# Forward transforms of three long convolutions in three F32R passes, with the first norm's x loaded in kernel row order

## The chip, the cores and the metric

The kernel runs on one core of one Trainium2 chip. The metric is the device time of one execution, in microseconds (us). A core has five engines that run side by side, each on its own list of instructions: TensorE (PE, with its weight loads shown apart as PEld), VectorE (DVE), ScalarE (ACT), GpSimd (POOL) and SyncE (SP). They wait for each other only where a semaphore says so. Transfers are issued by SP's and POOL's queues here and run on 16 DMA engines.

## The reference

One transformer-like block over 2048 rows of 576 channels: a norm with modulation, a long convolution (S4D) computed with FFTs, a residual, a second norm with modulation, a dense layer with ReLU (576 to 4608 to 576), a residual. All in float32.

```python
x = A_u
mod = (_silu(c) @ w_mod).reshape(c.shape[0], 6, 1, -1)
sa, ca, ga, sb, cb, gb = ...
h = _layernorm(x) * (1 + ca) + sa
# _A_ref: K[d, l] = 2 Re sum_n C exp(A dt l);  y = irfft(rfft(h) * rfft(K))[:L];  y + h * D_skip
x = x + ga * _A_ref(h, ...)
h = _layernorm(x) * (1 + cb) + sb
x = x + gb * (maximum(h @ w1, 0) @ w2)
```

## The kernel before

**Blocks.** The 2048 rows are four blocks of 512. For each block s there is a convolution `conv(s)` and a feed-forward part (FFN) of 36 groups, g = 36 s to 36 s + 35, 128 hidden channels each. A group is 14 products of 512 columns into `hps` (L1368), a ReLU on ScalarE (`hh`, L1373), the rest of it on VectorE (`hl`, L1374), and 14 products into the sums `acc` (L1394). Both FFN factors are split into high and low parts of type F32R, and a product is three passes: high times high, high times low, low times high. From group 110 on, the FFN's first half takes another form with 256-column products (`first2`, L1495).

**Order of the work.** conv(0) runs ahead of the FFN. What belongs to the later blocks is put between the FFN's products: `step`, called four times a group (144 steps a block), pulls pieces from a generator. Under block 0's FFN lie the kernel rotations of `rest` (the convolution kernels of the later blocks, L486 to L521) and then conv(1); under block 1's lie `finish(0)`, more of `rest`, and conv(2); under block 2's lie `finish(1)` and conv(3). A piece yields its estimated VectorE time, or `None` for a piece of TensorE work. A step pulls while the time pulled in the block is below `rate(b)` times the number of the step, while the last four steps have pulled less than 7.5 us (block 0) or 7.0 us, and at most two TensorE pieces. At the end of a block the rest is issued at once. The lists are then laid out by the scheduler of the Tile layer, which may reorder an engine's work; instructions wrapped in `Kept` keep their program order among themselves.

**The convolution.** conv(s) loads x of its block (`x2`, rows in the order m, n with row 4 m + n) and one of two kernel tiles `kt`, computes the first norm into `h` (`norm1`: statistics L903, two scalings L937 and L938), and transforms both by matrices: for each half p of the channels, `mm_K` transforms kernel rows with the table `fcK`, `mm_U` transforms `h` with `fcU`. One such call is `transform` (L847): eight float32 matmuls of 128 x 128 by 288 columns into `ps_f` (L854), each copied to `Z` on ScalarE (L855). There are four calls a convolution, interleaved with the butterflies (`butterfly`, L860 to L883) of the call before. The tables differ since the kernel rows lie in another order on the partitions than x: place j holds row group 8 (j mod 16) + j // 16. Then come the products over earlier blocks (`product`, L1034 to L1040, with tiles `T`), the inverse transforms into x (`inverse`, L1061, L1066), the second norm, transposes (L1155), and the split into `xh`, `xl`, `xs` (L1159 to L1168), on which the next block's FFN begins.

**Memory.** Big tiles of a convolution come from a ring of seven S tiles (`spec`, 9216 bytes a partition), small ones from two T tiles (`half`). The memory of the rings is opened anew for each convolution, on the place where the tables of `rest` were.

**Queues.** SP's queue carries the FFN's weights. POOL's queue carries x, the kernel tiles, the stored spectra (`Ud`, `Kd`, `Rd`) and the outputs, in program order where they are `Kept`.

Of the kernel before, what the change touches and what calls it, by code (L numbers as in the profile page):

```python
# [18 lines left out]
P = 128  # L19
# [556 lines left out]
class Body:  # L576
# [34 lines left out]
    def early(self, kg):  # L611

        nc, I, sm = self.nc, self.I, self.sm
        x2 = self.x2[0] = self.x2p[0].tile([P, 4, D], F32, tag="x2", bufs=1, name="x2_0")
        nc.sync.dma_start(out=x2, in_=I["x"][0:512, :].rearrange("(m n) d -> m n d", n=4))
        self.fcU, self.fcK, self.gc = (
            sm.tile([P, 4, 2, P], F32, name=n) for n in ("fcU", "fcK", "gc")
        )
        for t, n in ((self.fcK, "fck"), (self.fcU, "fcu"), (self.gc, "gc")):
            nc.sync.dma_start(out=t, in_=I[n])  # L620
        kept = self.tc.keep_in_program_order
        self.mv1 = mv = sm.tile([P, 4, 5], F32, name="mv1")
        for i in range(4):
            yield
            st = sm.tile([P, 2, 6], F32, tag="st", bufs=8, name="st0")
            for p in range(2):
                kept(nc.vector.bn_stats(out=st[:, p], in_=x2[:, i, p * PC : (p + 1) * PC]))
            kept(nc.vector.bn_aggr(out=mv[:, i, 0:2], in_=st))
        yield
        kept(nc.scalar.activation(mv[:, :, 2], mv[:, :, 1], AF.Sqrt, bias=self.eps))  # L630
        yield
        kept(nc.vector.reciprocal(mv[:, :, 3], mv[:, :, 2]))
        kept(nc.vector.scalar_tensor_tensor(
            mv[:, :, 4], mv[:, :, 0], -1.0, mv[:, :, 3], op0=ALU.mult, op1=ALU.mult
        ))
        self.h0 = h = kg.pw.tile([P, 4, D], F32, tag="W2", bufs=5, name="h_0")
        for i in (0, 2, 1, 3):
            kept(nc.scalar.activation(
                h[:, i], x2[:, i], AF.Identity, scale=mv[:, i, 3:4], bias=mv[:, i, 4:5]
            ))  # L640
        yield
        self.kt0 = kg.kt0
        kept(self.skip(self.kt0, 0, nc.vector))
        for i in (0, 2, 1, 3):
            kept(nc.vector.tensor_tensor(h[:, i], h[:, i], self.m["ca"], op=ALU.mult))
            kept(nc.vector.tensor_tensor(h[:, i], h[:, i], self.m["sa"], op=ALU.add))
        self.wm = {}
        for nm in ("sb", "cb"):
            self.wm[nm] = kg.pw.tile([P, 5, D], F32, tag="W2", bufs=5, name=f"wm_{nm}")
        yield  # L650
# [121 lines left out]
    def main(self, ctx, kg, hooks):  # L772
# [11 lines left out]
        def block0():  # L784
            self.x2p.append(self.pool(ctx, "x2b"))
            yield from kg.rest(
                self.cps, {h: (1, 2, 3) if h < 6 else (1,) for h in (0, 6, 1, 7, 2, 8, 3, 9, 4, 10, 5, 11)}
            )
            self.xp.append(self.pool(ctx, "xb"))
            pool(1)  # L790
            yield from self.conv(1)

        def block1():
            yield from self.finish(0)
            yield -1
            self.cvs.close()
            yield from kg.rest(self.cps, {h: (2, 3) for h in range(6, NH)})
            pool(2)
            yield from self.conv(2)

        def block2():
            yield from self.finish(1)
# [122 lines left out]
    def norm1(self, x2, h):  # L925
# [9 lines left out]
        for i in range(4):  # L935
# [2 lines left out]
            f(h[:, i], h[:, i], mv[:, 3:4], self.m["sa"], op0=ALU.mult, op1=ALU.add)  # L938
            yield 1.6

    def conv(self, s):

        nc = self.nc
        v = self.vec.tensor_tensor
        xp = self.xp[s % 2]
        if s:
            x2 = self.x2p[s % 2].tile([P, 4, D], F32, tag="x2", bufs=1, name=f"x2_{s}")
            self.x2[s] = x2
            Kept(self.tc, nc.gpsimd).dma_start(
                out=x2,  # L950
                in_=self.I["x"][s * 512 : (s + 1) * 512, :].rearrange("(m n) d -> m n d", n=4),
            )
        else:
            x2, h = self.x2[0], self.h0
            self.fcKn, self.gcn = (
# [8 lines left out]

        kt = [kernel_tile(0) if s else self.kt0, None]
        yield -1 if s else "mod"
        if s:
            h = self.spec(f"h_{s}").rearrange("p a b c -> p a (b c)")
        hv = h.rearrange("m n (dd p q) -> m n dd p q", dd=4, p=2)

        def mm_U(p, Z):
            return self.transform(lambda n2: hv[:, n2, :, p], self.fcU, Z, s == 0)

        def mm_K(p, Z):
            ktv = kt[p].rearrange("p (t dd g) q -> p t dd g q", t=2, g=2)
            if s == 0 and p == 1:
                self.skip(kt[p], p, Kept(self.tc, nc.gpsimd))
            src = lambda n2: ktv[:, n2 // 2, :, n2 % 2]
            if s == 0 and p == 1:
                return self.transform1(src, self.fcK, self.fcKn, Z)  # L980
            return self.transform(src, self.fcK, Z, s == 0)
# [112 lines left out]
            yield from mm_K(1, ZK)  # L1094
            self.save(self.Rd[0][0], Ks[0], Kept(self.tc, nc.gpsimd))
        else:
            yield from both(self.norm1(x2, h), mm_K(0, ZK))
            kt[1] = kernel_tile(1)
            ZU = self.spec("Z")
            yield from both(spec_K(0, ZK), mm_U(0, ZU))  # L1100
# [603 lines left out]
            yield  # L1704

    def rate(self, b):
        return (2.15, 1.8, 1.4, 0.5)[b]


def after(n, g):  # L1710
# [19 lines left out]
def _layout(inputs):  # L1730
# [3 lines left out]
    perm = np.arange(D).reshape(4, 2, 3, 2, 12).transpose(1, 2, 3, 0, 4).reshape(-1)  # L1734
    r = {}
    r["x"] = a["A_u"].reshape(L, D)
    for k, s in (("lar", "A_log_A_real"), ("ai", "A_A_imag")):
        x = a[s][perm].reshape(NH, H, N).transpose(1, 0, 2)
        r[k] = np.concatenate([x, np.zeros((KR - 2 * H, NH, N), x.dtype), x])
# [50 lines left out]
```

## Time and profile before

| | us |
|---|---|
| runs: median of 3 (lowest to highest) | 1319.47 (1313.34 to 1321.47) |
| the profiled execution | 1324.17 |
| its span, first to last instruction | 1322.4 |
| its mean granted TensorE clock | 0.943 |
| busy: PE, PEld, DVE, ACT, POOL | 1210.1, 973.6, 993.3, 518.8, 161.1 |

The profile is of one execution. Its views used here: the chain of work that ended last, busy time of each engine in chosen stretches (times from the span's start), groups of equal instructions, and single instructions in order of time. A group's row has, after the shapes and the count, its busy us and the mean ns of one, then the idle time before it with what ended it. In a row of the timeline, start and length come first, and the bracket at the end tells how long the engine had been idle and who released it. Matmuls overlap in the records, so that a single one looks longer than it costs; what one costs is read from a run of many.

### The profile page before, as it was taken

Reading aid. Unit: us, or ns where it says so; the run is one execution under the profiler, and the core shown is the slowest. Engines: PE = TensorE matmul, PEld = TensorE weight load, DVE = VectorE, ACT = ScalarE, POOL = GpSimd, SP = SyncE. Lnnn points to the kernel's source line nnn. Section 1 sums busy time; section 2 is a strip of 40 time slices with the busy share of each in tenths; the row PEclk is TensorE's granted clock in tenths of the full one; section 3 lists DMA queues with packets and bytes.
Section 4 is the critical chain, followed back from the end, with each engine's and each line's share of the span. In section 5 each row is a group of like instructions: output and inputs, shape, how many; then the busy total and the mean of one; then the engine's idle time right before and its main releaser. Section 6 shows DMA issues by size and latency. Waiting matters only on the chain.

```text
span 1322.4 us, 27077 instructions
## 1 busy us (share of the span) xinstructions
PE 1210.1 (92%) x11094; PEld 973.6 (74%) x11094; DVE 993.3 (75%) x1538; ACT 518.8 (39%) x902; POOL 161.1 (12%) x256
## 2 busy tenths in 40 slices
PE   4665586899989998999999999999999999999998
PEld 3454464677767787787677887887888888998997
DVE  7899988999986999689468995467997237555543
ACT  5788423222223422622243225433222365434431
POOL 1676411011000100110001000100000000000000
PEclk9556787999989999999899999999999999999999
DMA  9758972988878967799779995877996658666641
GB/s 273 269 201 307 327 275 79 351 289 321 312 267 294 344 228 274 249 405 343 251 266 340 348 353 155 274 220 263 373 388 191 180 166 256 190 190 190 193 142 63
DMA packets 118032, 343.81 MB, mean 260 GB/s; under 512 B 17772, under 2 KB 21652, under 8 KB 107156
## 3 DMA queue, kind: packets, MB, share of 16 engines
q1 hardware_dynamic: 101332, 226.04, 51.0%
q0 software_dynamic: 16064, 114.67, 22.9%
q8 instruction: 87, 1.43, 0.4%
q10 hardware_dynamic: 512, 1.38, 0.3%
q14 instruction: 37, 0.30, 0.1%
HBM read 260.63 MB, written 81.40 MB: 259 GB/s over the span
## 4 chain that ended last, share of the span: by engine, by line
PE 71%; DVE 16%; DMA 7%; issue 3%; ACT 1%; POOL 1%; SPq 0%; ACTq 0%; DVEq 0%
PE acc L1394 28%; PE hps L1368 21%; PE hps L1495 7%; PE ps_f L854 5%; DMA L1d<-w 4%; PE kps L73 2%; PE kps L521 2%; PE ps_i L1061 2%; PE ph L73 2%; DVE T L486 1%; DVE W1r L488 1%; DMA x<-in_x_dram 1%; DVE Y L1040 1%; DVE T L64 1%; DVE w L1338 1%
## 5 line engine op out<-in xcount | busy, mean ns | idle before, releaser
L1394 PE MATMUL acc<-w,hh 128*128 128x512 f32 x1008 | 323.1, 403 | 3.2 <-ACT hh L1373 2.7
L1368 PE MATMUL hps<-xh,w 128*128 128x512 f32 x880 | 307.4, 410 | 0.7 <-ACT xh L49 0.7
L1394 PEld LDWEIGHTS acc<-w,hh 128*128 128x128 f32 x1008 | 187.4, 188 | 44.0 <-ACT hh L1373 3.6
L1368 PEld LDWEIGHTS hps<-xh,w 128*128 128x128 f32 x880 | 168.6, 192 | 38.7 <-ACT xh L49 1.3
L1394 PE MATMUL acc<-w,hl 128*128 128x512 f32 x504 | 195.1, 401 | 1.5 <-DVE hl L1374 1.5
L1343 ACT ACTIVATE w<-r 128x576 fp32r<-128x576 f32 x141 | 96.6, 685 | 229.7 <-PE acc L1394 195.2
L1368 PE MATMUL hps<-xl,w 128*128 128x512 f32 x440 | 175.7, 400 | 0.0
L1373 ACT ACTIVATE hh<-hps 128x512 fp32r<-128x512 f32 x110 | 65.7, 597 | 242.1 <-PE hps L1368 237.4
L1374 DVE SCALAR_TENSOR_TENSOR hl<-hps,hh 128x512 fp32r<-128x512 f32 x110 | 75.4, 685 | 113.1 <-ACT hh L1373 112.5
L1394 PEld LDWEIGHTS acc<-w,hl 128*128 128x128 f32 x504 | 94.3, 189 | 22.8 <-DVE hl L1374 3.0
L1333 ACT ACTIVATE w<-r 128x640 fp32r<-128x640 f32 x124 | 90.8, 732 | 42.7 <-DMA L1d<-w 42.1
L1368 PEld LDWEIGHTS hps<-xl,w 128*128 128x128 f32 x440 | 84.1, 191 | 18.3 <-DVE xl L49 0.4
L1040 DVE TENSOR_TENSOR Y<-Y,T 128x1152 f32<-128x1152 f32 x60 | 79.3, 1348 | 0.0
L73 PE MATMUL kps<-W,W 128*32 128x16 f32 x2304 | 39.4, 210 | 42.8 <-POOL W L70 28.4
L1368 PE MATMUL hps<-xs,w 128*128 128x512 f32 x220 | 78.0, 421 | 0.0
L855 ACT ACTIVATE Z<-ps_f 128x288 f32<-128x288 f32 x120 | 49.0, 410 | 71.6 <-PE ps_f L854 69.7
L73 PEld LDWEIGHTS kps<-W,W 128*32 128x32 f32 x2304 | 34.7, 142 | 56.4 <-POOL W L70 31.0
L521 PEld LDWEIGHTS kps<-W1r,W2r 128*32 128x32 f32 x3456 | 45.1, 113 | 38.8 <-issue 20.8
L521 PE MATMUL kps<-W1r,W2r 128*32 128x48 f32 (+2 forms) x3456 | 52.4, 202 | 15.9 <-ACT ker L531 9.3
L1503 DVE TENSOR_TENSOR C<-C,hps 128x256 f32<-128x256 f32 x17 | 7.1, 420 | 63.0 <-PE hps L1495 63.0
L1394 PE MATMUL acc<-hh,w 128*128 128x512 f32 x126 | 50.7, 402 | 0.0
L1394 PE MATMUL acc<-hl,w 128*128 128x512 f32 x126 | 49.9, 396 | 0.0
(307 smaller groups left out, 2197.9 us busy)
## 6 DMA issues: line engine op xcount, KB each, us to landing
r<-in_w_dram SPq DMA_DIRECT2D x144, 320.0 KB, 3.9
r<-in_w_dram SPq DMA_DIRECT2D x144, 288.0 KB, 4.9
w<-L2d SPq DMA_DIRECT2D x108, 288.0 KB, 4.1
w<-L1d SPq DMA_DIRECT2D x92, 320.0 KB, 3.9
W2r<-W2d POOLq DMA_DIRECT2D x18, 1536.0 KB, 8.5
W2d<-W SPq DMA_DIRECT2D x12, 1536.0 KB, 8.5
Ua<-Ud POOLq DMA_DIRECT2D x15, 1152.0 KB, 9.5
W<-W1d POOLq DMA_DIRECT2D x18, 768.0 KB, 9.4
```

Source lines behind the costliest of these rows:

```text
L73: self.tc.keep_in_program_order(self.nc.tensor.matmul(*args, **kw))
L521: nc.tensor.matmul(ps[32 * dd : 32 * dd + 32, q, :], W2[:, r, ch], W1[:, r, ch], start=(r == 0), stop=(r == 1),)
L854: nc.tensor.matmul(o, fc[:, n2, c, :], src(n2), start=True, stop=True)
L855: ev = nc.scalar.activation(Z[:, n2, c], ps[:, :PC], AF.Copy)
L1040: v(y, y, T, op=op or ALU.add)
L1333: copy(g - 1)(w1[g][:, 0], r1[g], AF.Copy)
L1343: copy(g)(w[:, 0:D], r2[g], AF.Copy)
L1368: nc.tensor.matmul(ps, a, x, start=(i == 0), stop=(i == 13))
L1373: nc.scalar.activation(hh, ps, AF.Relu)
L1374: nc.vector.scalar_tensor_tensor(hl, ps, 0.0, hh, op0=ALU.max, op1=ALU.subtract)
L1394: nc.tensor.matmul(acc[i], a, x, start=(f == 0 and seen[i] == 1), stop=(f == NF - 1 and seen[i] == (3 if i < 4 else 2)),)
L1495: nc.tensor.matmul(out, l, m, start=(i == 0), stop=(i == len(ops) - 1))
```

## The change

For the last three convolutions (s = 1, 2, 3) the forward transforms no longer use one float32 matmul but three F32R matmuls on high and low parts, as the FFN does. conv(0) is left as it is.

- The table `fcK` is split once, at the start of conv(1) (`table`): a ScalarE copy to F32R (`fch`, in the memory of `fcU`), a subtraction on VectorE, a ScalarE copy to F32R (`fcl`, in the memory of `fcK`).
- Before each transform its input is split (`split`): two ScalarE copies and two VectorE subtractions of 576 elements a partition, into the two T tiles. `thirds` then runs the 24 matmuls and eight copies to `Z`.
- `h` and the kernel rows use the same table. For that, x for the first norm comes from a new input `xk`, whose rows are in the kernel's order, loaded straight into the S tile of `h` (`load_h`), and `norm1` works in place. The load stands before conv(1) and conv(2), and for conv(3) after conv(2).
- `x2`, still needed for the inverse and the residual, is loaded after the first norm and the first transform.
- The rates are 2.22, 1.86, 1.46 instead of 2.15, 1.8, 1.4, and each half of a split yields 0.8, the table 1.5.

```diff
         self.fcU, self.fcK, self.gc = (
-            sm.tile([P, 4, 2, P], F32, name=n) for n in ("fcU", "fcK", "gc")
+            sm.tile([P, 4, 2, P], F32, tag=n, bufs=1, name=n) for n in ("fcU", "fcK", "gc")
         )
...
             pool(1)
+            self.load_h(1)
             yield from self.conv(1)
...
             pool(2)
+            self.load_h(2)
             yield from self.conv(2)
+            self.load_h(3)
...
+    def load_h(self, s):
+
+        h = self.spec(f"h_{s}").rearrange("p a b c -> p a (b c)")
+        Kept(self.tc, self.nc.gpsimd).dma_start(
+            out=h.rearrange("m n d -> m (n d)"), in_=self.I["xk"][s - 1]
+        )
+        self.h = {s: h}
+
...
-        if s:
+        def load_x():
             x2 = self.x2p[s % 2].tile([P, 4, D], F32, tag="x2", bufs=1, name=f"x2_{s}")
             self.x2[s] = x2
             Kept(self.tc, nc.gpsimd).dma_start(
...
+            return x2
+
+        if s:
+            h = self.h.pop(s)
...
-        if s:
-            h = self.spec(f"h_{s}").rearrange("p a b c -> p a (b c)")
...
+        def split(x, name):
+            hi, lo = (
+                self.half(name + n).rearrange("p n (a b) -> p n a b", a=4).bitcast(F32R)
+                for n in "hl"
+            )
+            for i in range(2):
+                h, l = (t[:, 2 * i : 2 * i + 2] for t in (hi, lo))
+                nc.scalar.activation(h, x[i], AF.Copy)
+                v(l, x[i], h, op=ALU.subtract)
+                yield 0.8
+            return lambda n2: (hi[:, n2], lo[:, n2])
+
+        def table():
+            f = lambda t: t.rearrange("p n c k -> p (n c k)")
+            sm, shape = self.sm, [P, 4, 2, P]
+            hi = sm.tile(shape, F32R, tag="fcU", bufs=1, name="fch")
+            nc.scalar.activation(f(hi), f(self.fcK), AF.Copy)
+            t = self.spec("fct").rearrange("p a b c -> p (a b c)")[:, :1024]
+            v(t, f(self.fcK), f(hi), op=ALU.subtract)
+            yield 1.5
+            lo = sm.tile(shape, F32R, tag="fcK", bufs=1, name="fcl")
+            nc.scalar.activation(f(lo), t, AF.Copy)
+            self.parts = hi, lo
+
+        def thirds(p, Z, x, name):
+            hi, lo = self.parts
+            src = yield from split(x, name)
+            for n2 in (0, 2, 1, 3):
+                xh, xl = src(n2)
+                for c in range(2):
+                    ps = self.cps.tile([P, 512], F32, tag="cps", bufs=self.nps, name="ps_f")
+                    o = ps[:, :PC].rearrange("p (a b) -> p a b", a=4)
+                    fh, fl = hi[:, n2, c], lo[:, n2, c]
+                    for i, (a, b) in enumerate(((fh, xh), (fh, xl), (fl, xh))):
+                        nc.tensor.matmul(o, a, b, start=(i == 0), stop=(i == 2))
+                    nc.scalar.activation(Z[:, n2, c], ps[:, :PC], AF.Copy)
+                    yield None
+
         def mm_U(p, Z):
+            if s:
+                return thirds(p, Z, [hv[:, 2 * i : 2 * i + 2, :, p] for i in range(2)], "hs")
             return self.transform(lambda n2: hv[:, n2, :, p], self.fcU, Z, s == 0)
...
+            if s:
+                x = kt[p].rearrange("p (t dd g) q -> p t g dd q", t=2, g=2)
+                return thirds(p, Z, [x[:, i] for i in range(2)], "ks")
...
-            yield from both(self.norm1(x2, h), mm_K(0, ZK))
+            if s == 1:
+                yield from table()
+            yield from both(self.norm1(h, h), mm_K(0, ZK))
+            x2 = load_x()
             kt[1] = kernel_tile(1)
...
-        return (2.15, 1.8, 1.4, 0.5)[b]
+        return (2.22, 1.86, 1.46, 0.5)[b]
...
+    x = r["x"].reshape(NB, 16, 8, 4 * D).transpose(0, 2, 1, 3).reshape(NB, P, 4 * D)
+    r["xk"] = x[1:]
```

## The prediction, made before the changed kernel was run

> **What bounds the kernel now.** First the span and the chain that ended last, then busy time by stretch, then single instructions.
>
> ```profile
> span 1322.4 us, 27077 instructions
> ...
> PE 71%; DVE 16%; DMA 7%; issue 3%; ACT 1%; POOL 1%; SPq 0%; ACTq 0%; DVEq 0%
> ```
>
> The profiled execution took 1324.17 us, 4.7 above the median of the runs (1319.47), so I sum against 1324.17 and take 4.7 off at the end. The chain is mostly TensorE, but 16% of VectorE means stages with another limit. The blocks of the feed-forward part (FFN) end where ScalarE copies the last sum out (L1634):
>
> ```profile
> 545.82 0.58 ACT L1634 ACTIVATE o<-acc 128x512 f32<-128x512 f32 x1
> ...
> 833.05 0.59 ACT L1634 ACTIVATE o<-acc 128x512 f32<-128x512 f32 x1
> ...
> 1091.04 0.59 ACT L1634 ACTIVATE o<-acc 128x512 f32<-128x512 f32 x1
> ```
>
> Convolution 1 lies under block 0 (until 546), 2 under block 1, 3 under block 2. Stretches cut at their steps (columns: stretch, length, then busy us with instruction counts of PE, PEld, DVE, ACT, POOL, then clock, DMA share, GB/s):
>
> ```profile
> 400.00:421.00 21.00, 21.00 (x185) 17.51 (x180) 11.31 (x34) 6.21 (x13) 0.54 (x1) 1.00 0.94 348
> 421.00:457.00 36.00, 36.00 (x146) 25.14 (x145) 33.05 (x53) 17.51 (x39) 3.87 (x6) 1.00 0.80 290
> 457.00:528.00 71.00, 67.80 (x285) 53.82 (x284) 69.89 (x96) 19.38 (x32) 3.73 (x7) 0.98 0.73 263
> 528.00:553.00 25.00, 24.55 (x119) 19.08 (x118) 17.25 (x46) 17.85 (x34) 0.00 (x0) 1.00 0.72 230
> ...
> 630.00:654.00 24.00, 21.31 (x441) 15.87 (x440) 13.88 (x29) 5.81 (x14) 2.22 (x4) 0.89 0.72 247
> 654.00:723.00 69.00, 69.00 (x288) 53.11 (x288) 43.39 (x59) 26.67 (x55) 7.08 (x11) 0.99 0.84 296
> 723.00:833.00 110.00, 110.00 (x490) 89.75 (x489) 83.57 (x114) 41.20 (x69) 4.28 (x8) 1.00 0.81 285
> 833.00:924.00 91.00, 91.00 (x393) 72.36 (x393) 58.25 (x95) 36.59 (x76) 7.69 (x14) 1.00 0.76 254
> ```
>
> The transforms that change (L854) stand in 421-457, 654-723 and 833-924. In the last two TensorE never rests and VectorE has 25 and 33 us to spare: **TensorE sets the time of blocks 1 and 2**. In 421-457 both are full (VectorE 33 of 36), and in 457-528, where the products follow, VectorE is busy 69.9 of 71: **VectorE sets the time of block 0's convolution**. The same transform is worth its TensorE time in one place and its VectorE time in the other.
>
> **The price of one transform, before.** In 842.97-920.84 TensorE does only transforms and FFN products; these rows count them (L854, L1368, L1394), and then come one FFN run and a run of 256-column products (L1495):
>
> ```profile
> 842.97:920.84 77.87, 19.88 (x60) 1.00 0.74 250
> 842.97:920.84 77.87, 38.58 (x140) 1.00 0.74 250
> 842.97:920.84 77.87, 36.28 (x132) 1.00 0.74 250
> ...
> 943.10 3.17 PE hps L1368 x14
> ...
> 1123.64:1129.58 5.94, 5.94 (x50) 1.00 0.59 180
> ```
>
> A 512-column product of F32R tiles takes 3.17/14 = 0.2267 us. The 272 of them make 61.7; the other 16.2 us are 60 records, and as each F32 matmul leaves two, 30 transforms: **0.54 us each**.
>
> **After:** three F32R products of 288 columns. No such product is in the trace; it lies between 256 columns (5.94/50 = 0.1188) and 512 (0.2267), so three cost between 0.356 and 0.680. By the line between the two rows, near the lower one, one costs 0.1323, three 0.397. That saves 0.143 a transform, 32 x 0.143 = 4.6 us a convolution and 13.7 for all 96; the ends are 17.7 saved and 13.4 lost.
>
> One rule speaks against it. The Trainium skill ("TensorE: Matmul & The Clock Gate", Part 3, The mechanism) says that a weight load overlaps running matmuls only where the row groups differ, and its section on LDWEIGHTS puts 128 columns at about 107 ns. By it three full-height products with a load each would come to an estimated 3 x 0.239 = 0.72 us, a loss. The 50 products above, each with a load of its own, show 0.1188 for the pair, so here the trace disagrees; the rule is kept as a rival below.
>
> **The splits.** Each of the four transforms of a convolution gets two ScalarE copies and two VectorE subtractions of 576 elements; the table is split once, with 1024 elements. Nearest rows:
>
> ```profile
> L868 DVE TENSOR_TENSOR W<-Z 128x576 f32<-128x576 f32 x24 | 18.1, 753 | 17.8 <-ACT Z L855 17.7
> L1338 DVE TENSOR_TENSOR w<-r,w 128x640 fp32r<-128x640 f32 x33 | 26.9, 814 | 0.7 <-ACT w L1333 0.7
> L1458 DVE TENSOR_TENSOR S<-Sr,S 128x1024 fp32r<-128x1024 f32 x17 | 20.9, 1226 | 4.8 <-ACT S L1457 4.8
> L1343 ACT ACTIVATE w<-r 128x576 fp32r<-128x576 f32 x141 | 96.6, 685 | 229.7 <-PE acc L1394 195.2
> L1457 ACT ACTIVATE S<-Sr 128x1024 fp32r<-128x1024 f32 x17 | 18.0, 1059 | 6.1 <-PE hps L1495 6.1
> ```
>
> VectorE: 8 x 0.75 = 6.0 us a convolution, and 1.2 for the table. ScalarE: 8 x 0.685 = 5.5, and 2.1. ScalarE is busy at most half of any stretch above but 528-553, which holds no split: its share costs nothing, though each split adds a copy and a subtraction ahead of its transform (about 1.4 us a half). There are two T tiles, and a split fills both, so the next split waits until the last transform has read them. TensorE has FFN work meanwhile; without it each of three such gaps would cost up to 2.9 us.
>
> **Block 0.** VectorE gets 7.2 us more where it sets the time. The table falls into 400-421, where it idles 9.7 us, and perhaps some of the first split. The higher rate ends the kernel rotations about three of 144 steps sooner, and the later steps carry their FFN work on VectorE instead: no net work. I count the yields: the convolution now ends at step 140 instead of 135, nearer the block's end, so its last part (528-553: inverse, second norm, transposes) has fewer FFN products beside it. But those are what it queues behind, so what is lost by less cover is part won by less crowding. Of 6 us I take 4 as staying, less 2 for VectorE's waits for transforms in 421-457 (3 us idle), which get shorter: **+2**. The ends: -4.6 if TensorE were the limit, +9 if all 7.2 and a 2 us gap stay.
>
> **Blocks 1 and 2.** Splits: 6.0 us of VectorE each into 25 and 33 us of idle time in their own stretches. Saved: 2 x 4.6 = **-9.2**. Block 1's convolution has some 10 us of slack: its last xl (L1168) starts at 823.3, the block ends at 833. The block shortens by 4.6, so a convolution up to 5 us later still fits; past that every us counts.
>
> ```profile
> 823.27 0.69 DVE L1168 TENSOR_TENSOR xl<-xf,xh 128x512 fp32r<-128x512 f32 x1 [0.64 <-ACT xh L1161]
> ```
>
> **x and its moved loads.** The norm now reads a tile loaded in kernel row order and rewrites it in place: same instructions, same sizes. Three more loads of 1152 KB go out on POOL's queue, 0.53 us of issue each, and x itself is loaded later, after the first transform, ahead of the second kernel tile's load; nothing needs it before the inverse. DMA is at 0.72 to 0.84 there. Block 1 shows what a late load costs:
>
> ```profile
> x<-in_x_dram POOLq DMA_DIRECT2D x3, 1152.0 KB, 12.7
> ...
> 630.40 0.53 POOL L49 DMA_DIRECT2D x<-in_x_dram  x1
> 632.86 1.18 POOL L1291 DMA_DIRECT2D kt<-kd  x1 [1.92 <-issue]
> 653.90 0.54 POOL L841 DMA_DIRECT2D R<-Rd  x1 [19.86 <-PE kps L521]
> ...
> 644.49 2.26 DVE L903 BATCH_NORM_STATS2 st<-x 128x6 f32<-128x288 f32 x6 [5.33 <-DMA x<-in_x_dram]
> 646.66 0.67 DVE L1374 SCALAR_TENSOR_TENSOR hl<-hps,hh 128x512 fp32r<-128x512 f32 x1
> ...
> 649.33 0.95 PE L521 MATMUL kps<-W1r,W2r 128*32 128x32 f32 x48 [2.69 <-ACT ker L531]
> ```
>
> The statistics stand ahead of hl on VectorE and wait for x until 644.5; TensorE rests 2.7 us before 649.3 and then runs some 14 products at about half speed, by the 0.89 of the stretch: about 6 us in all. The new load has the same place, so the stall stays: 0, with ends of -6 (gone) and +11 (below). Block 2's load is moved ahead, into block 1's end; TensorE is full there either way: 0.
>
> **Sum:** -9.2 + 2 + 0 = -7.2, that is 1317.0 for an execution like the profiled one and **1312.3 us** for the median. A difference of about 1%, 13.2 us, is what a measurement of this kernel tells from no change.
>
> **Rivals.**
> 1. TensorE's time counts everywhere and block 1's stall goes: -13.7 - 6, so 1299.8. For it: TensorE is full in 421-457 too, and the scheduler may order the statistics behind hl. Against: 69.9 of 71 us VectorE.
> 2. The splits eat the gain: +9 in block 0, so 1319.3. For it: block 0 has no slack, its convolution ends as the block does. Against: 9.7 us idle in 400-421.
> 3. Slower: the new tile lies in the ring of S tiles, and that memory was the kernel rotations'. R, also an S tile, waited 19.9 us for the last of them. If the new load has to wait likewise, it starts near 648 instead of 630.4 (653.9 less the 6 us stall), the statistics follow 17.5 later, and hl behind them stops TensorE. With 6 us of FFN work to go on with, 11 more are lost: -7.2 + 11, so 1323.3; if nothing covers it, 17.5, and with rival 2's block 0 (+7 more) 1337. It decides from a wait of about 7 us on. Against: the first S slot may lie where only early tables were.
> 4. Weight loads do not overlap: a load shows 0.19 (row below), so three products become 3 x 0.32 = 0.97, or +41 us for 96 transforms, 1360. The row of 50 products speaks against it. By the rule of the Trainium skill quoted above ("TensorE: Matmul & The Clock Gate") it would be an estimated +17. That the split does not bring the fast form at all (0.68, +13.4) belongs here too: 1333.
>
> ```profile
> L1394 PEld LDWEIGHTS acc<-w,hl 128*128 128x128 f32 x504 | 94.3, 189 | 22.8 <-DVE hl L1374 3.0
> ```
>
> **How the numbers follow.** Forecast 0.48 (its own range 1306 to 1318), rival 1 0.22, rival 2 0.20, rival 3 0.08, rival 4 0.02. Faster by over 1% (below 1306.3): most of rival 1 (0.20) and the forecast's lower edge (0.05). Slower by over 1% (above 1332.7): half of rival 3 and the upper edge of rival 2 (0.08), rival 4 (0.02). The range reaches from near rival 1 to past rivals 2 and the milder 3: 1301 to 1325.
>
> **What would show it.** Right: in the stretches of transforms in blocks 1 and 2 three products take about 0.40 us, and blocks 1 and 2 together shorten by 8 to 10 us; block 0 ends (first L1634) 0 to 5 us later than 545.8; its 70 us of products stay at 98% VectorE. Wrong: a 288-column product of 0.18 us or more; statistics of convolution 2 that wait over 10 us for their load; a first L1634 before 542; or blocks 1 and 2 with TensorE gaps that wait for a split.

## The result and the profile after

The changed kernel takes 1334.57 us, the median of 6 runs (1330.66 to 1337.76), beside 1320.47 for 6 runs of the kernel before: ratio 1.0114, 95% interval 1.0093 to 1.0136. It is **slower by 1.1%**, where 1312.3 was forecast. The profiled execution took 1335.31 us. Its span and chain, from the page:

```profile
span 1333.5 us, 27335 instructions
...
PE 65%; DVE 22%; DMA 5%; issue 5%; ACT 2%; POOL 1%; SPq 0%; ACTq 0%; DVEq 0%; POOLq 0%
```

VectorE's share of the chain rose from 16% to 22%. The FFN blocks end here (ScalarE's timeline; L1693 is L1634 of before):

```profile
557.43 0.57 ACT L1693 ACTIVATE o<-acc 128x512 f32<-128x512 f32 x1
...
847.50 0.59 ACT L1693 ACTIVATE o<-acc 128x512 f32<-128x512 f32 x1
...
1102.95 0.59 ACT L1693 ACTIVATE o<-acc 128x512 f32<-128x512 f32 x1
```

The first FFN product started at 218.8 (221.4 before). So block 0 takes 338.7 instead of 324.4 us (+14.3), block 1 290.1 instead of 287.2 (+2.8), block 2 255.5 instead of 258.0 (-2.5). With 2.7 less ahead of block 0 and 0.8 less behind block 2 that makes the 11.1 between the two profiled executions.

Block 0 by the steps of convolution 1: forward transforms, from there to the last spectral sum, and the rest. First before, then after (columns as in the prediction's stretches):

```profile
421.20:460.80 39.60, 39.60 (x160) 27.57 (x159) 36.65 (x57) 19.15 (x42) 4.40 (x7) 1.00 0.82 301
460.80:521.10 60.30, 57.10 (x240) 45.67 (x239) 59.19 (x79) 15.71 (x25) 3.19 (x6) 0.97 0.73 261
521.10:545.80 24.70, 24.25 (x109) 18.92 (x107) 18.57 (x48) 12.68 (x24) 0.00 (x0) 1.00 0.79 264
```

```profile
422.80:475.00 52.20, 46.41 (x220) 35.82 (x220) 42.58 (x71) 25.04 (x53) 4.91 (x8) 0.93 0.73 261
475.00:537.50 62.50, 58.72 (x247) 46.71 (x247) 62.12 (x81) 15.71 (x25) 3.19 (x6) 0.97 0.80 281
537.50:557.40 19.90, 17.75 (x74) 12.94 (x72) 16.23 (x43) 8.92 (x18) 0.00 (x0) 1.00 0.77 251
```

The transforms start at nearly the same time and take 12.6 us longer. VectorE is busy 5.9 us more in them, and idle 9.6 us where it was 3.0. What it waited for, after:

```profile
DVE ksl L992 <- ACT ksh L991: 3.9, 1, 3.9
DVE W L871 <- ACT Z L1019: 3.3, 1, 3.3
DVE hsl L992 <- ACT hsh L991: 1.9, 2, 1.2
```

A subtraction of a split (L992) stands in VectorE's queue in the order written, and there it waits for ScalarE's copy; all behind it wait too. The worst place, in the timelines of ScalarE, VectorE and TensorE:

```profile
455.81 0.74 ACT L1392 ACTIVATE w<-r 128x640 fp32r<-128x640 f32 x1 [4.37 <-DMA L1d<-w]
...
456.87 0.76 DVE L871 TENSOR_TENSOR W<-Z 128x576 f32<-128x576 f32 x1 [3.30 <-ACT Z L1019]
...
463.56 0.76 DVE L992 TENSOR_TENSOR ksl<-kt,ksh 128x576 fp32r<-128x576 f32 x1 [3.92 <-ACT ksh L991]
...
456.89 0.61 PE L1018 MATMUL ps_f<-hsh,fch 128*128 128x288 f32 x1 [4.74 <-ACT Z L1019]
...
453.00:463.00 10.00, 6.11 (x22) 5.20 (x23) 3.33 (x6) 3.11 (x7) 0.00 (x0) 0.66 0.98 367
```

ScalarE's copy of a weight (w) waited for the store of the part that lay in its buffer; the transform's copy out of PSUM (Z) stood behind it, with it VectorE, and with that TensorE. For 10 us VectorE worked 3.3 and TensorE 6.1, at a granted clock of 0.66.

### The profile page after: what moved, and what is told of

It is laid out like the page before. It is cut to its first block, busy times and chain, and to the rows that moved or that the text cites. A ratio compares the mean times of both kernels' runs of the same rounds, so it can differ in the third digit from the quotient of the medians.

```text
span 1333.5 us, 27335 instructions
## 1 busy us (share of the span) xinstructions
PE 1207.4 (91%) x11190; PEld 974.7 (73%) x11190; DVE 1006.2 (75%) x1563; ACT 535.3 (40%) x928; POOL 162.0 (12%) x259
## 4 chain that ended last, share of the span: by engine, by line
PE 65%; DVE 22%; DMA 5%; issue 5%; ACT 2%; POOL 1%; SPq 0%; ACTq 0%; DVEq 0%; POOLq 0%
PE acc L1453 26%; PE hps L1427 18%; PE hps L1554 7%; PE ps_f L1018 3%; DVE T L1094 3%; DMA L1d<-w 3%; PE kps L521 2%; PE kps L73 2%; DVE Y L1096 2%; DVE W1r L488 2%; PE ph L73 2%; DVE T L486 2%; PE ps_i L1117 2%; DMA Ua<-Ud 1%; PE ps_f L857 1%
## 5 line engine op out<-in xcount | busy, mean ns | idle before, releaser
L1453 PE MATMUL acc<-w,hh 128*128 128x512 f32 x1008 | 315.2, 396 | 2.5 <-DVE w L1409 1.4
L1427 PE MATMUL hps<-xh,w 128*128 128x512 f32 x880 | 299.0, 400 | 0.7 <-ACT xh L49 0.7
L1453 PE MATMUL acc<-w,hl 128*128 128x512 f32 x504 | 191.1, 398 | 4.2 <-DVE hl L1433 4.2
L1019 ACT ACTIVATE Z<-ps_f 128x288 f32<-128x288 f32 x96 | 39.0, 407 | 49.7 <-PE ps_f L1018 49.0
```

Of the source, the lines that this page charges most:

```text
L1427: nc.tensor.matmul(ps, a, x, start=(i == 0), stop=(i == 13))
L1453: nc.tensor.matmul(acc[i], a, x, start=(f == 0 and seen[i] == 1), stop=(f == NF - 1 and seen[i] == (3 if i < 4 else 2)),)
```

## The experiments

Four theories for the loss. **L**: the moved loads and the memory they now lie on are late. **V**: VectorE's subtractions take their time in a stage that VectorE sets. **T**: a split fills both T tiles, which the spectral products use too, so each waits for the other. **Q**: ScalarE's queue, where a weight copy waits for its store. S, in the first expectations, is that the products wait for copy and subtraction in turn.

The profiles are compared by four lengths, each read from the one profiled execution of a kernel: A, from the first transform product of convolution 1 to the end of block 0; C, from the same product to the last `xl` of convolution 1 (L1168, L1227); then block 1 and block 2. In the five kernels whose convolution 1 has float32 transforms and the old loads (before, e2, e8, e11, e17), A is 124.3 to 124.8; in the four with float32 transforms and the moved loads (e1, e12, e16, e18) it is 125.7 to 127.1. So a difference of 2 us counts, and one of 1 us does not. The way from the first FFN product to the first transform varies more (199.8 us before, 204.0 after; 195 to 205 over all kernels) and is left aside here; the expectations still count block 0 from the first FFN product, which is A and this way together.

C is needed because A ends with the block and not with the convolution: the last `xl` comes 6.5 us after the block's end before the change, and 11.1 us after it in the changed kernel. Its rows, before, after, in e3 and in e7:

```profile
552.34 0.68 DVE L1168 TENSOR_TENSOR xl<-xf,xh 128x512 fp32r<-128x512 f32 x1
...
568.51 0.69 DVE L1227 TENSOR_TENSOR xl<-xf,xh 128x512 fp32r<-128x512 f32 x1 [0.91 <-ACT xh L1220]
...
560.33 0.69 DVE L1222 TENSOR_TENSOR xl<-xf,xh 128x512 fp32r<-128x512 f32 x1 [1.20 <-ACT xh L1215]
...
571.55 0.69 DVE L1227 TENSOR_TENSOR xl<-xf,xh 128x512 fp32r<-128x512 f32 x1 [0.49 <-ACT xh L1220]
```

| kernel | ratio to before, 95% interval | A | C | block 1 | block 2 |
|---|---|---|---|---|---|
| before | 1 | 124.6 | 131.1 | 287.2 | 258.0 |
| changed | 1.0114 (1.0093 to 1.0136) | 134.6 | 145.7 | 290.1 | 255.5 |
| e1 moved loads, no splits | 1.0001 (0.9981 to 1.0021) | 125.8 | 132.3 | 283.8 | 258.0 |
| e2 three passes in 2 and 3 | 0.9965 (0.9943 to 0.9988) | 124.4 | 130.9 | 283.0 | 255.9 |
| e3 no subtractions | 1.0003 (0.9982 to 1.0023) | 125.9 | 137.5 | 284.9 | 255.5 |
| e4 kernel tile first | 1.0149 (1.0122 to 1.0175) | 137.6 | 149.2 | 293.3 | 255.4 |
| e5 subtractions not read | 1.0071 (1.0045 to 1.0097) | 133.4 | 144.9 | 285.0 | 255.5 |
| e6 subtractions on GpSimd | 1.0106 (1.0069 to 1.0142) | 134.1 | 146.1 | 290.8 | 255.4 |
| e7 old rates | 1.0110 (1.0068 to 1.0151) | 128.1 | 145.4 | 290.6 | 259.5 |
| e8 as e2, block 1 paced faster | 0.9990 (0.9963 to 1.0018) | 124.5 | 131.0 | 285.4 | 255.4 |
| e9 splits in S tiles | 1.0082 (1.0050 to 1.0114) | 132.4 | 144.0 | 286.4 | 256.3 |
| e10 as e9, no subtractions | 1.0049 (1.0031 to 1.0067) | 129.7 | 141.0 | 286.7 | 255.5 |
| e11 as e2, splits in S tiles | 0.9987 (0.9955 to 1.0020) | 124.3 | 130.8 | 284.5 | 255.4 |
| e12 three passes in 3 alone | 0.9984 (0.9964 to 1.0004) | 125.7 | 132.2 | 282.3 | 255.3 |
| e13 early stores | 1.0106 (1.0067 to 1.0145) | 133.1 | 144.2 | 290.3 | 255.4 |
| e14 early stores, S tiles | 1.0080 (1.0052 to 1.0107) | 133.3 | 145.2 | 289.7 | 255.4 |
| e15 as e14, no subtractions | 1.0030 (1.0012 to 1.0048) | 127.4 | 139.2 | 286.9 | 257.0 |
| e16 early stores, no splits | 0.9991 (0.9969 to 1.0014) | 126.8 | 133.3 | 282.3 | 258.0 |
| e17 as e2, early stores | 0.9960 (0.9932 to 0.9987) | 124.8 | 131.3 | 282.5 | 255.9 |
| e18 as e12, early stores | 0.9967 (0.9945 to 0.9989) | 127.1 | 133.7 | 283.3 | 255.3 |

**One part alone.** e1 takes the splits out, the table's too, and leaves the loads moved; with the splits gone it also has the old rates (so has e16, while the kernels with three passes in some convolutions only have them for the blocks of the others):

```
-  return thirds(p, Z, [hv[...], ...], "hs")
-  return thirds(p, Z, [x[:, i] ...], "ks")
+  return self.transform(lambda n2: hv[:, n2, :, p], self.fcK if s else self.fcU, Z, s == 0)
   ...
-  return (2.22, 1.86, 1.46, 0.5)[b]
+  return (2.15, 1.8, 1.4, 0.5)[b]
```

> The changed kernel without the splits: every forward transform is again two float32 products, the moved loads stay (h in kernel row order into the first S slot, x later from the new input), and the rates are the old ones. Theory L (the loads and the memory they now lie on are late, so the convolutions start late): block 0 still ends 8 to 12 us later than the 545.8 of before, the next kernel tile's load of block 1 still comes some 30 us late, and the whole takes 1330 to 1340 us. Theory V (the splits' 7 us of VectorE work and their waits in a stage that VectorE bounds): block 0 ends at 543 to 549, and the whole is 1316 to 1324 us.

Theory L falls: 1.0001. A is 1.2 longer, and block 1 is 3.4 shorter, since its stall is gone: h comes in time, TensorE waits there for nothing but a 1.3 us stop for hl.

e2 keeps convolution 1 as before the change, with its old loads and rate (`if s > 1` in place of `if s`).

> Three passes in the last two convolutions only; the first of the three is as before the change (its h in transform order, x loaded early, float32 transforms), so block 0's end should be the 545.8 of before within 2 us in either theory. What is left is the change in blocks 1 and 2. If TensorE's saving comes through there as forecast (4.6 us each): 1309 to 1313 us. If block 1 loses what it lost in the changed kernel (+2.8 us where -4.6 was forecast) and block 2 gains 2.5: 1319 to 1322 us.

Block 1 is 283.0, no more than the 283.8 that the loads alone bring: TensorE's saving does not show there. Block 2 gains 2.1. The whole is 0.35% faster than before (0.12 to 0.57%), and 1.5% faster than the changed kernel: convolution 1 is where the change costs.

**Subtractions.** e3 leaves them out, and e5 makes them, but no product reads their result:

```
-  v(l, x[i], h, op=ALU.subtract)                    (e3)
-  return lambda n2: (hi[:, n2], lo[:, n2])          (e3, e5)
+  return lambda n2: (hi[:, n2], hi[:, n2])
```

> The changed kernel with VectorE's subtraction of each split left out: the high part stands in for the low part in the products, so the low part of the input does not enter the result; ScalarE's copies, the products and all loads are the same. Theory V: the 5 or 6 us of subtractions in each convolution come back in block 0, which ends 6 to 10 us earlier than the 557.4 of the changed kernel; whole 1322 to 1328 us. Theory L: block 0 ends within 3 us of 557.4 and the whole is 1331 to 1336 us. Theory S (the splits come one at a time, ScalarE's copy and VectorE's subtraction in turn, and the products wait on that): between the two, 3 to 6 us.

> The changed kernel with VectorE's subtractions made as they are, into the same tiles, but the low products read the high part instead, so the low part of the input does not enter the result and no product waits for a subtraction. Block 0 lost 14 us from its first product on (338.7 against 324.4), and 10.4 of them went when the subtractions were left out. Theory V (VectorE's own time for them, 5.4 us, is what costs): block 0 from first product to end stays at 336 to 339 us and the whole at 1331 to 1336. Theory S (the products wait for copy and subtraction in turn): block 0 takes 328 to 332 and the whole is 1321 to 1327. Half each: 333 to 335.

Without the subtractions the whole loss is gone (1.0003): A falls by 8.7 us, C by 8.2, block 1 by 5.2. Copies and three products alone leave A where the loads alone have it (125.9 against 125.8), but convolution 1 is still longer by 5.2 us of C (137.5 against 132.3) and runs that much further into block 1; this does not show in the whole. VectorE waits there 4.9 us for ScalarE's copies out of PSUM (Z), in e1 1.0. With the subtractions made but unread (e5), A stays at 133.4. That would speak against S in block 0, but it is not a clean test: the subtractions of e5 wait 6.1 us for T tiles, in the transforms, which those of the changed kernel do not. Block 1 takes 285.0 in e5, as without them. And e3 uses one T tile where the changed kernel uses two, so V and T are not yet apart.

e6 moves the subtractions to GpSimd (`nc.gpsimd.tensor_tensor(l, x[i], h, ...)`).

> The changed kernel with the splits' 24 subtractions of inputs on GpSimd instead of VectorE; the chain of copy, subtraction and product stays, with whatever GpSimd takes for one. Theory V: block 0 from first product to end 331 to 335 us instead of 338.7, the whole 1325 to 1330. Theory S: block 0 stays at 337 to 343, and the whole at 1332 to 1340, more if GpSimd takes over 1.5 us for one.

V expected 4 to 8 us back; block 0 from its first product is 335.3, but A only 0.5 shorter, and the whole is that of the changed kernel within its interval. This does not speak for S: VectorE was not relieved, because those of its own instructions that ran beside GpSimd's got longer. Groups of GpSimd, then of VectorE, in 415 to 480 and 419 to 471:

```profile
L992 POOL TENSOR_TENSOR hsl<-h,hsh 128x576 fp32r<-128x576 f32 x4 | 11.9, 2997 | 13.6 <-ACT hsh L991 13.6
L992 POOL TENSOR_TENSOR ksl<-kt,ksh 128x576 fp32r<-128x576 f32 x4 | 7.0, 1756 | 19.9 <-ACT ksh L991 19.9
...
L872 DVE TENSOR_TENSOR W<-Z 128x576 f32<-128x576 f32 x6 | 7.0, 1158 | 0.0
L871 DVE TENSOR_TENSOR W<-Z 128x576 f32<-128x576 f32 x6 | 6.6, 1096 | 4.8 <-ACT Z L1019 4.8
...
L940 DVE SCALAR_TENSOR_TENSOR h<-h,mv,m_ca 128x576 f32<-128x576 f32 x3 | 4.7, 1564 | 0.0
...
L1059 DVE SCALAR_TENSOR_TENSOR K<-R,sgn,K 128x1152 f32<-128x1152 f32 x1 | 2.6, 2574 | 0.0
```

In the changed kernel the same VectorE groups took 752 to 754, 811 and 1414 ns (mean of one).

**Order and pacing.** e4 gives the kernel tile its memory and its place in the queue ahead of h; e7 has the old numbers `(2.15, 1.8, 1.4, 0.5)`; e8 is e2 with 2.05 instead of 1.86 for block 1.

> The changed kernel with one thing moved: the kernel tile takes its memory and its place in the queue ahead of h, as x and the kernel tile's load stood in the kernel before. Theory L for block 1: the kernel tile's load of conv 2, at 667 us in the changed kernel, is issued at 633 to 645 again, the transforms start 10 to 18 us earlier, and block 1 is 3 to 7 us shorter than 290.1; block 0 gains 0 to 4 us; whole 1326 to 1332 us. Theories V and S: within 2 us of the changed kernel's 1334.6, since the splits are untouched.

> The changed kernel with the pacing numbers of before (2.15, 1.8, 1.4 instead of 2.22, 1.86, 1.46). Theories V, S and L alike: the rates carry little; whole within 4 us of 1334.6, block 0 within 2 us of 557.4. If the higher rates were the cause (they put splits and products into earlier steps): block 0 ends 5 us or more earlier and the whole is below 1329.

> Three passes in the last two convolutions only, as in the run of that kind (1315.5), with block 1's pacing number at 2.05 instead of 1.86. There the last part of convolution 2 ended 1.1 us before its block's end, where before it had 9.8. If that lateness comes from the pacing (the splits are counted as steps): convolution 2 ends 5 us or more before the block, block 1 takes 280 to 282 us instead of 283.0, the whole 1312.5 to 1315. If VectorE itself sets it (60.5 of 65 us in the products): block 1 within 1 us of 283.0, the whole 1314.5 to 1317.

e4 is no faster: the kernel tile's load of convolution 2 goes out at 646 instead of 667 us, but the transforms start 126.9 us after block 0's end, in the changed kernel 127.5, and block 1 is longer by 3.2, so L falls a second time. In e7 A is 6.5 us shorter, as if the rates were the cause, but C is that of the changed kernel (145.4): convolution 1 takes as long, and only the block's end falls earlier in it. Block 2 takes 4.0 us more, and the whole stays (1.0110). So the rates move the loss between blocks and do not make it. In e8 the last `xl` of convolution 2 started 4.1 us before the end of its block instead of 1.1, and block 1 was no shorter (285.4): the pacing is not what costs there.

**T tiles and the late store.** e9 puts a split's two parts into an S tile, e10 is e9 without subtractions, e11 is e2 with S tiles, and e12 has three passes in convolution 3 alone:

```
-  hi, lo = (self.half(name + n)... for n in "hl")
+  t = self.spec(name)
+  hi, lo = (t[:, :, i]... for i in range(2))
```

> The changed kernel with each split's two parts in one of the seven S tiles instead of the only two T tiles, which the products also use; work and order are the same. Theory T (a split fills both T tiles, so the next split waits for the products of the last, and the spectral products wait for the last split's): the transforms of convolution 1 take 43 to 47 us instead of 52.2, block 0 from its first product 329 to 334 instead of 338.7, block 1 284 to 287 instead of 290.1; whole 1321 to 1328. Theory V (VectorE's 5.4 us of subtractions, wherever they lie): block 0 336 to 339, block 1 289 to 291, whole 1331 to 1336. The S ring may bring waits of its own, which would show as DVE or DMA waits for S tiles.

> As the run with the splits in S tiles, and the subtractions left out (products read the high part in place of the low one, so the low part of the input does not enter the result). Against that run it takes away VectorE's work alone, with the tiles equal. Theory V: block 0 is 5 to 8 us shorter than there. Theory T: at most 2 us shorter there, since VectorE then has room.

> Three passes in the last two convolutions only (1315.5), with the splits in S tiles. There the spectral products of convolution 2 waited 4.7 us for a T tile and its last part ended 1.1 us before the block. Theory T: that wait is gone, convolution 2 ends 5 us or more before its block; block 1 280 to 282 us against 283.0; whole 1312.5 to 1315.5. Theory V: no change, 1315 to 1317.

> The run without splits (moved loads, float32 transforms; 1319.9) with three passes in the last convolution alone, where TensorE was full and VectorE has 33 us of idle time. TensorE's saving by the spacing in the trace, 0.49 against 0.40 us a transform, is 3 us for 32 of them: block 2 255 to 256 us instead of 258.0, blocks 0 and 1 as there (325.9 and 283.8) within 2 us, whole 1316 to 1318. By the 0.54 us of the prediction, 4.6 us: block 2 253.4.

In e9 block 0 from its first product is 332.8, as T expected, but 3.6 of the 5.9 us lie on the way to the first transform: A is 132.4, the transforms take 50.1 where T promised 43 to 47, and the whole (1332.5) is as V had it. So T is about 2 us of A, at the edge of what counts. The S tiles also bring a wait of their own, as the expectation feared: in convolution 2 VectorE waits 5.4 us for a store of U (5.4 in e11, 6.6 in e14), and not in the changed kernel. In e10 block 0 takes 334.7, longer than e9's where V had it 5 to 8 shorter; in A it is 2.7 shorter. There the weight copy waited 5.4 us for its store within the transforms, in e9 0.9, so the two were not alike and Q came up. e11 is no faster than e2. In e12 block 2 gives 2.7, as the spacing in the trace had it, not 4.6.

So e13 to e16 put the store right behind the subtraction that makes it, ahead of the next loads on SyncE's queue; e13 is the changed kernel, e14 e9, e15 e10 and e16 e1 with that edit:

```
-  for dst, src in late: nc.sync.dma_start(...)      (behind load_r1, load_r2)
   ...
   lo1(g + 2)
+  for dst, src in late: nc.sync.dma_start(...)
   low1(g + 3)
```

> The changed kernel with the stores of the weights' low parts (L1d, L2d) put on SyncE's queue right behind the subtractions that make them, ahead of the next step's loads instead of behind them. Nothing else differs. In the changed kernel ScalarE's copy w waited 4.4 us for such a store at 451 to 456, with the copies of transforms and splits queued behind it, and VectorE worked only 3.3 of the next 10 us. Theory Q (that queue is a part of the loss): the wait is gone, VectorE has no such hole, block 0 from first product to end takes 330 to 334 us instead of 338.7, the whole 1326 to 1331. Theories V and T alone: block 0 336 to 339, whole 1332 to 1337.

> Splits in S tiles and the early stores together. Theories T and Q both right: block 0 328 to 332 us (332.8 with the S tiles alone), whole 1320 to 1327; what is then left over the 325.9 of the run without splits is VectorE's work. If the S tiles had already taken the hole away, 332 to 334.

> As the run with S tiles and early stores, and without the subtractions (high part in place of the low one, so the input's low part does not enter the result). The difference between the two is VectorE's work alone, with no T tile and no late store in the way. Theory V: block 0 4 to 6 us shorter than with the subtractions, 325 to 328. If VectorE's work does not count: within 1.5 us of it. In the run with S tiles and late stores this block took 334.7, with a 5.4 us wait of the copy w; theory Q says 6 or more of them go.

> The control: early stores in the run without splits (block 0 325.9, whole 1319.9), where no w copy waits within the transforms. All theories: block 0 within 2 us of 325.9 and the whole within 3 of 1319.9. If the early stores help by themselves (there w waits 11.6 us behind the products), block 0 is 3 us or more shorter.

From the first FFN product e13's block 0 is 333.9, 4.8 shorter and within what Q expected; but the control e16 gains 2.9 there too (323.0), since the way to its first transform is 4 us shorter. In A, e13 is 133.1 and e14 133.3. In e14 no weight copy waits for a store or a load within the transforms, and in e16 one waits 4.4 us (for its load) and A is only 1.0 longer than e1's. So **Q falls** as the cause: the wait at 451 to 456 was a place where lateness showed.

With neither T tiles nor late stores in the way, leaving out the subtractions takes 133.3 - 127.4 = 5.9 us off A and 6.0 off C, and brings the whole from 1.0080 to 1.0030, with intervals that just do not meet. **V stands**: 5.9 is close to their own time, 8 of 0.754 us. Three things stay open. The same step with late stores (e9 to e10) took off only 2.7 of A. Leaving out the subtractions also ends the products' wait for the low parts, so this pair does not tell V from S. And e15 itself is not free: its C is nearly 6 us longer than that of e16, which has no splits, and VectorE waits 6.3 us for Z, in e16 1.7. Its whole is 1.0030 against 0.9991, with intervals that just meet. So the copies and their place in ScalarE's queue lengthen convolution 1 too, and no run takes that part by itself. Transforms of e14 and e15:

```profile
419.70:469.80 50.10, 43.17 (x194) 33.29 (x193) 43.78 (x79) 23.19 (x50) 4.90 (x8) 0.90 0.69 247
```

```profile
419.50:465.90 46.40, 42.92 (x211) 33.25 (x209) 38.91 (x72) 23.72 (x53) 4.44 (x8) 0.96 0.87 307
```

Last, the versions that these runs point to:

> Three passes in convolutions 2 and 3 only, convolution 1 as before the change, and the early stores. If the account holds (block 1 keeps the gain of the moved loads, block 2 gains 2.5, block 1 loses TensorE's 2.5 again to VectorE's waits): blocks 322 to 324, 282 to 284, 255 to 256, whole 1312 to 1316. If the late stores hide a wait that the splits of convolution 2 cause: block 1 279 to 281, whole 1309 to 1312.

> Three passes in convolution 3 alone, moved loads and early stores: blocks 323, 282 and 255.5, whole 1313 to 1316. Against the run beside it this tells what the splits of convolution 2 bring: if VectorE's waits eat TensorE's saving there, the two are equal within 1.5 us; if the saving comes through in block 1, this one is 2.5 us slower.

Both are faster than both kernels, by 0.40% (0.13 to 0.68%) and 0.33% (0.11 to 0.55%) against before; e17's median was 1312.97 us. With the splits of convolution 2 block 1 takes 282.5, without 283.3: they bring nothing that can be measured.

## Why the prediction was wrong

**The price of a transform.** Three products do overlap their weight loads. TensorE's timeline after:

```profile
886.34 0.29 PE L1018 MATMUL ps_f<-hsh,fch 128*128 128x288 f32 x1
886.47 0.29 PE L1018 MATMUL ps_f<-hsl,fch 128*128 128x288 f32 x1
886.60 0.29 PE L1018 MATMUL ps_f<-hsh,fcl 128*128 128x288 f32 x1
886.73 0.62 PE L1427 MATMUL hps<-xs,w 128*128 128x512 f32 x2
...
893.04 0.37 PE L1018 MATMUL ps_f<-hsh,fch 128*128 128x288 f32 x1
893.24 0.29 PE L1018 MATMUL ps_f<-hsl,fch 128*128 128x288 f32 x1
893.38 0.29 PE L1018 MATMUL ps_f<-hsh,fcl 128*128 128x288 f32 x1
893.50 0.39 PE L1453 MATMUL acc<-w,hh 128*128 128x512 f32 x1
```

A triple takes 0.39 us as forecast (886.34 to 886.73) in 23 of the 32 of block 2, and 0.46 to 0.51 in nine, where the second product came 0.20 us after the first instead of 0.13 (as at 893.04); the mean is 0.42. The rest of the error lies in the 0.54 of before: block 2 is 2.5 us shorter, 0.08 for each of 32, so a float32 transform cost about 0.50. TensorE's timeline before agrees:

```profile
852.42 0.65 PE L854 MATMUL ps_f<-kt,fcK 128*128 128x288 f32 x2
852.69 0.83 PE L1368 MATMUL hps<-xs,w 128*128 128x512 f32 x2
853.37 0.40 PE L1368 MATMUL hps<-xh,w 128*128 128x512 f32 x1
```

From 852.42 to 853.37 TensorE does one transform and two FFN products of 0.23 us, so the transform is 0.49; nine of the 32 cost 0.55 to 0.73. The count of records was complete. What it had too low is the FFN product: the 0.2267 us is from a run of FFN products alone, and in this stretch they stood 0.2298 apart (mean of 214), so that 272 of them took 0.8 us more, 0.03 for each of the 30 transforms. The mechanism was right and **the term of -4.6 a block is -2.5** in block 2.

**Block 0, "+2".** This is the step that failed: the block took 14.3 us more. The step took 6 us as VectorE's price, let 4 of them stay, and took off 2 for waits that would get shorter. The price was right to the digit (groups after, whole kernel):

```profile
L992 DVE TENSOR_TENSOR hsl<-h,hsh 128x576 fp32r<-128x576 f32 x12 | 9.0, 754 | 8.8 <-ACT hsh L991 8.8
L992 DVE TENSOR_TENSOR ksl<-kt,ksh 128x576 fp32r<-128x576 f32 x12 | 8.9, 754 | 7.8 <-ACT ksh L991 7.8
```

but each subtraction also waits, with the engine's whole queue behind it: the same rows show 16.6 us of idle time ahead of 17.9 us of work. VectorE's idle time in the transforms did not shrink from 3 us, it grew to 9.6. Nor was there much to shrink: of the 3 us before, only 0.2 were a wait for a transform (Z), the rest for ScalarE's hh and for a load:

```profile
DVE hl L1374 <- ACT hh L1373: 1.4, 2, 1.2
DVE T L1038 <- DMA Ua<-Ud: 1.2, 1, 1.2
DVE W L868 <- ACT Z L855: 0.2, 1, 0.2
```

Nor did the idle time ahead of them take anything up: VectorE is busy 10.1 of 400-421 after, 11.3 before. The table's subtraction fell there as forecast (1.2 us), but some of the weights' subtractions and the norm's last small steps left it, and the statistics came 16.6 us later, with idle time ahead of them. A is 10.0 longer: 1.2 with the loads (e1) and 8.7 with the subtractions (e3). Of C's 14.6 us the loads make 1.2, copies and three products 5.2, the subtractions 8.2; some 6 of the last are about their own time (e14 and e15), and the rest, waits around them and for T tiles, is not taken apart. The other 4.3 of the 14.3, on the way to the first transform, are not settled; kernels that differ little are as far apart.

```profile
400.00:421.00 21.00, 21.00 (x95) 17.33 (x93) 10.14 (x23) 6.47 (x11) 1.71 (x2) 1.00 1.01 382
```

"ScalarE's share costs nothing" was true of its time (25.0 of 52.2 us) and not of its order: VectorE waits for its copies, and C grows by 5.2 us in e3 without any subtraction.

**Block 1, -4.6.** It grew by 2.8. The stall is gone (-3.4 in e1) and TensorE saves 2.5, so 8.7 came in elsewhere. Two holes of TensorE, in the timelines and in ninths of the block:

```profile
557.40:589.60 32.20, 29.60 (x133) 23.80 (x134) 18.57 (x24) 16.62 (x28) 6.38 (x12) 0.95 0.61 231
...
783.00:815.30 32.30, 29.17 (x121) 23.59 (x121) 28.11 (x25) 8.35 (x14) 0.11 (x1) 0.95 0.85 329
...
808.35 1.20 PE L1453 MATMUL acc<-w,hl 128*128 128x512 f32 x4 [3.13 <-DVE hl L1433]
...
734.61 2.63 DVE L1094 TENSOR_TENSOR T<-K,Ua 128x1152 f32<-128x1152 f32 x2 [5.93 <-PE ps_f L1018]
```

The first is the end of convolution 1, which runs into block 1. The second is VectorE, late with hl; ahead of it the products of convolution 2 had waited 5.9 us for a T tile that the last split held until its last product. The holes are 2.6 and 3.1 us, 5.7 of the 8.7; the granted clock of 0.95 in these two ninths (1.00 in both before) would make an estimated 3 more (5% of 64.5 us). "25 us of idle time" were not there for the taking, and the 10 us of slack went: the last xl started 4.1 us before the end of the block in the changed kernel and 1.1 in e2, instead of 9.8. Whether the T tile matters for block 1 stays open: e5, in which the low part's tile is free once written, has no such wait for T and 285.0, and e9 has 286.4, but e14, with S tiles as well, has 289.7.

**x and its moved loads, 0.** Right for the whole (e1: 1.0001), but partly by luck, since the forecast had its parts otherwise: the stall of block 1 did go, as rival 1 had it (block 1 is 3.4 shorter), and A grew by 1.2. The wait of rival 3 came, in convolution 1:

```profile
390.76 0.53 POOL L49 DMA_DIRECT2D h<-in_xk_dram  x1 [17.84 <-PE kps L521]
...
416.89 2.97 DVE L906 BATCH_NORM_STATS2 st<-h 128x6 f32<-128x288 f32 x8
```

The statistics moved from 400.3 to 416.9, still ahead of their use (the first scaling starts at 420.1, before at 420.7). So rival 3's time, 1323 to 1337, holds the result, but not by its mechanism. **Rival 2** named the mechanism, at +9 in block 0, with too small a sum since the gain it was set against was half as large, and block 1 lost too.

Of the signs named in advance: a first L1693 at 557.4 was outside the 0 to 5 us, and blocks 1 and 2 together changed by +0.3 instead of -8 to -10. Product price, statistics of convolution 2 (no wait) and the 98% of VectorE in the products (62.12 of 62.5) held.

## What to carry to other kernels

An instruction added to the engine that sets a stage can cost its own time in full, and more if it needs another engine's result first, since the queue behind it waits too: count for each added pair of copy and subtraction the gap between them, and credit no idle time that lies ahead of the inputs' arrival. Where work is spread over steps, measure a stage to its own last instruction: a boundary such as a block's end can move within it. Put a saving of one engine only where that engine is the limit and the other has slack to the end of the stage: of three convolutions, only the last one gained. And where a price is worked out as a remainder, take the price of the rest from the same stretch, and check it against the spacing of single rows.

## What the runs showed of the hardware

GpSimd's two-input subtractions made VectorE's two-input instructions beside them longer: in the mean of a group 1096 to 1158 instead of 752 to 754 ns, 1564 instead of 811 and 2574 instead of 1414 (e6 against the changed kernel). They themselves took 1.76 us (kernel rows) and 3.0 us (h) in the mean where VectorE takes 0.75; so the work did not leave VectorE by being moved. The Trainium skill ("SBUF — State Buffer", SBUF: two separate sides) says that VectorE and GpSimd share one pair of ports, which for instructions like these, with two inputs in SBUF, one of them holds for a whole instruction. The trace of e6 agrees: a W of VectorE that started at 449.53, within a GpSimd subtraction of 449.28 to 450.70, took 1.79 us.

After the gap of 4.7 us ahead of 456.89, shown above, TensorE's products of 288 columns came 0.24 us apart instead of 0.13, for some 4 us at a granted clock of 0.50:

```profile
457.30 0.44 PE L1018 MATMUL ps_f<-hsl,fch 128*128 128x288 f32 x1
457.54 0.44 PE L1018 MATMUL ps_f<-hsh,fcl 128*128 128x288 f32 x1
457.78 1.48 PE L1453 MATMUL acc<-w,hl 128*128 128x512 f32 x3
...
457.00:461.00 4.00, 4.00 (x12) 3.48 (x13) 2.64 (x5) 0.95 (x3) 0.00 (x0) 0.50 0.98 367
```
